# Weight sums moved one block earlier, second-layer weight halves fetched first, token tiles spread: an attention recurrence with two MLPs on one core

## The chip, the cores and the metric

One Trainium2 chip, of which the kernel uses one core. The metric is device microseconds of one execution, as the median of several runs. Lower is better.

## The reference

A linear-attention recurrence feeds a first MLP with a leaky rectifier, and that feeds a second, gated MLP:

```python
for t in range(S):                      # B=4, H=8, S=768, D=48
    cur = einsum('bhd,bhe->bhde', u * k[t], v[t])
    y[t] = einsum('bhd,bhde->bhe', r[t], state + cur)
    state = w * state + einsum('bhd,bhe->bhde', k[t], v[t])
x = y.transpose(0, 2, 1, 3).reshape(3072, 384)
h = x @ w_in                            # 384 -> 2048
x = (maximum(h, 0) + alpha * minimum(h, 0)) @ w_out      # 2048 -> 384
out = ((x @ w1) * (x @ w2)) @ w3 @ w_out2     # 384 -> 1024 -> 1024 -> 384
```

The weights arrive as 64-bit floats. The kernel converts them on the chip into a high and a low 32-bit half, and every product of the MLPs is made of three matmuls (high by high, low by high, high by low), in the helper `mm3` (L123 to L126).

## The kernel before, in words

**Blocks.** The 768 time steps are cut into 6 blocks of 128 steps. With 4 batches that is 512 columns a block, the width of nearly every matmul. A block holds 4 units of attention (a unit is a pair of heads). While the first MLP works on block i, the attention units of block i+1 are woven into its steps.

**The order of the work is written by hand.** A block of the first MLP has 16 steps f, one for each 128 of the 2048 hidden channels. Lists of words say what is issued in a step: `P` is `product1` (9 matmuls into one of two PSUM banks `ph`), `r` is `relus` (two ScalarE passes that free the bank), `s` is `slope` (VectorE), `hl` is `halves` (a ScalarE cast and a GpSimd subtraction, through `split` L120, L121), and `D3` is `down1` of three steps earlier (9 matmuls into `acc`). The list `MIDDLE` (blocks 1 to 4, a period of 4 steps, one attention unit in each period) also holds the words of attention; the list `LAST` (block 5, where no attention is left) is `hl1 P r s D3 xx`. Every engine runs its own instructions in the order in which they were issued, and SP, which issues nearly all DMAs, is one such queue too.

**The word `xx`** runs the function `extra` once in each step of the last block, and all that prepares the second MLP stands in it:

- `mix_load`, `mix`, `mix_store` (L460 to L483): for each of 8 groups of channels two loads of 256 KB, six VectorE operations that make sums and differences of weights, a split into halves by ScalarE and GpSimd, and four stores. The second MLP needs these sums because it forms its products by a scheme that saves matmuls.
- `fetch_o2(k)` (L485 to L494): one of 8 pieces of the second `w_out`, 384 KB each, with both of its halves.
- `fetch_3(j)` (L496 to L503): 1 MB of w3, as tiles `w3h` (of the pool tag "rk", two buffers) and `w3l`; `fold(j)` (24 matmuls of 384 columns into `pf`) multiplies it with all 8 pieces of `w_out`, so that w3 and `w_out` become one matrix; `folded(j)` splits the result `m`. The folds lie in the steps 4 to 11. The two `fetch_3` of the first folds are issued as the block begins, the others two folds ahead.
- `fetch_12(q)` (L451 to L453): weights w of the second MLP, 384 KB, into the buffer of a `w_in` tile that is used up.
- `load_x2`, `x_sum`, `x_cast`, `x_low`, `x_both` (L655 to L716): token tiles of the second MLP (`xr`), their sums (`xsum`, of the tag "rk" as well) and halves (`x`, `xc`), 6 of them ahead of the second MLP's first products.

**The second MLP**, `second`, follows. Its products into the banks `pq` stand in `times` (L753); a copy `t<-pq` (L774) by ScalarE frees the first bank.

**A block's attention** ends with `put_h` and `put_l`, which turn a unit's output y into the halves x, and `put_done`, whose two DMAs `x<-e` (L366) bring them in place. The unit's tiles `rk` and `nat` are loaded by L173 and L174.

The few lines that set the order:

```python
LAST = ("hl1 P r s D3 xx",)
...
words = (MIDDLE, MIDDLE, MIDDLE, MIDDLE, LAST)[i - 1]
for word in words[f % len(words)].split():
```

Of the kernel before, what the change touches and what calls it, by code (L numbers as in the profile page):

```python
# [7 lines left out]
F32 = mybir.dt.float32  # L8
F32R = mybir.dt.float32r
# [8 lines left out]
P = 128  # L18
C = 128
NB = S // C  # L20
NHP = H // 2
N = B * C
DM = H * D
KD = DM // P
F1 = 2048
F2 = 1024
M1 = F1 // P
M2 = F2 // P
# [40 lines left out]
AHEAD2 = ("x11", "x00-x11", "x01+x11", "x00", "x21", "x20")  # L69
# [3 lines left out]
def tile_kernel(ctx: ExitStack, tc: tile.TileContext, a: dict, out: bass.AP):  # L73
    nc = tc.nc
# [4 lines left out]
    gp = ctx.enter_context(tc.tile_pool(name="gp", bufs=GB))  # L79
    ld = ctx.enter_context(tc.tile_pool(name="ld", bufs=2))  # L80
    wk = ctx.enter_context(tc.tile_pool(name="wk", bufs=1))
    st = ctx.enter_context(tc.tile_pool(name="st", bufs=4))
    cv = ctx.enter_context(tc.tile_pool(name="cv", bufs=2))
# [35 lines left out]
    def split(dst_h, dst_l, src, lo=None):  # L119
        nc.scalar.copy(out=dst_h, in_=src)  # L120
        (lo or nc.gpsimd).tensor_tensor(out=dst_l, in0=src, in1=dst_h.bitcast(F32), op=ALU.subtract)  # L121
# [267 lines left out]
    parts = {}  # L389
# [38 lines left out]
    wo2 = {}  # L428
# [22 lines left out]
    def fetch_12(q):  # L451
        w2s[q] = x = wts.tile([P, 2, KD, P], F32R, tag=f"wi{q % M1}", name=f"w12_{q}")
        nc.sync.dma_start(out=x.bitcast(F32).rearrange("p s c m -> p (s c m)"), in_=s12[q % SLOTS])  # L453

    mixes = {}

    def seen(f, j, c0, c1):
        return s12[3 * f + j].rearrange("p (s c m) -> p s c m", s=2, c=KD)[:, :, c0:c1]

    def mix_load(f):  # L460
        mixes[f] = parts = [wk.tile([P, 2, 2, P], F32, tag="rs", name="mix", bufs=2) for j in range(2)]
        for j in range(2):
            nc.sync.dma_start(out=parts[j], in_=seen(f, j, 0, 2))

    def mix(f):
        parts = mixes[f]
        t, o = (wk.tile([P, 4, P], F32, tag=x, name="mix") for x in ("ks", "q1"))
        op = nc.vector.tensor_tensor
        for j in range(2):
            op(out=t[:, 2 * j:2 * j + 2], in0=parts[j][:, 0], in1=parts[j][:, 1], op=ALU.add)  # L470
        w00, w01, w10, w11 = (t[:, m] for m in range(4))
        op(out=o[:, 0], in0=w11, in1=w10, op=ALU.subtract)
        op(out=o[:, 1], in0=o[:, 0], in1=w01, op=ALU.add)
        op(out=o[:, 2], in0=o[:, 1], in1=w00, op=ALU.subtract)
        op(out=o[:, 3], in0=w01, in1=w11, op=ALU.add)
        mixes[f] = h, l = [gp.tile([P, 4, P], F32R, tag="o", name="mix", bufs=3) for _ in range(2)]
        split(h, l, o)

    def mix_store(f):
        for s, x in enumerate(mixes.pop(f)):  # L480
            x = x.bitcast(F32)
            nc.sync.dma_start(out=seen(f, 2, 0, KD)[:, s], in_=x[:, 0:KD])
            nc.sync.dma_start(out=seen(f, 1, 1, 2)[:, s], in_=x[:, KD:])  # L483

    def fetch_o2(k):  # L485
        if k < 7:
            pool, tag, bufs = ((st, "raw", 4), (wk, "am", 2), (wk, "e", 1))[(k >= 4) + (k >= 6)]
            x = pool.tile([P, 2, DM], F32R, tag=tag, name=f"wo2{k}", bufs=bufs)
            nc.sync.dma_start(out=x.bitcast(F32).rearrange("p s m -> p (s m)"), in_=so2[k])
            wo2[k] = x[:, 0], x[:, 1]  # L490
        else:
            wo2[k] = [cv.tile([P, DM], F32R, tag="t", name=f"wo2{k}") for _ in range(2)]
            for m, x in enumerate(wo2[k]):
                nc.sync.dma_start(out=x.bitcast(F32), in_=so2[k, :, m * DM:(m + 1) * DM])  # L494
        ready.add(("o2", k))

    def fetch_3(j):
        w3[j] = (
            ld.tile([P, M2, P], F32R, tag="rk", name="w3h"),
            ld.tile([P, M2, P], F32R, tag="nat", name="w3l"),  # L500
        )
        for m, x in enumerate(w3[j]):
            nc.sync.dma_start(out=x.bitcast(F32).rearrange("p k m -> p (k m)"), in_=s3[j, :, m])  # L503
        ready.add(("w3", j))

    late = [False]
# [138 lines left out]
    def folded(j):  # L645
        m = wts.tile([P, 2, DM], F32R, tag=f"wo{j}", name=f"m{j}")
        split(m[:, 0], m[:, 1], pfs.pop(j), nc.vector)
        ms[j] = m
# [3 lines left out]
    xr = {}  # L652
    xs = {}

    def load_x2(p):  # L655
        for c in range(KD):
            tag, bufs = ("am", 2) if c < 2 else ("e", 1)
            xr[p, c] = raw = wk.tile([P, 2, N], F32, tag=tag, name="xr", bufs=bufs)
            nc.sync.dma_start(out=raw, in_=x2d[2 * p:2 * p + 2, :, c].rearrange("b p n -> p b n"))

    NAMES = ("x11", "x00-x11", "x01+x11", "-x10-x11", "x00+x01", "x00+x10", "x00", "x21", "x20")
# [19 lines left out]
    def x_part(p, x):  # L681
        return xr[p, int(x[1])][:, int(x[2])]

    def x_sum(p, name):
        k = NAMES.index(name)
        if k in (1, 3, 5):
            xt2[p, k] = ld.tile([P, 2, N], F32, tag="rk", name="xsum")
        s = xt2[p, k] if k in (1, 3, 5) else xt2[p, k - 1]
        s = s[:, k in (2, 4)]
        xs[p, name, "sum"] = s  # L690
        if name[0] == "-":
            nc.vector.scalar_tensor_tensor(
                out=s, in0=x_part(p, name[1:4]), scalar=-1.0, in1=x_part(p, name[5:]), op0=ALU.mult, op1=ALU.subtract
            )
        else:
            nc.vector.tensor_tensor(
                out=s, in0=x_part(p, name[:3]), in1=x_part(p, name[4:]), op=ALU.add if name[3] == "+" else ALU.subtract
            )

    def x_cast(p, name):  # L700
        src = x_part(p, name) if len(name) == 3 else xs.pop((p, name, "sum"))
        h, l = xs[p, name] = x_home(p, NAMES.index(name))
        nc.scalar.copy(out=h, in_=src)  # L703
        xs[p, name, "src"] = src

    def x_low(p, name, e=None):
        h, l = xs[p, name]
        (e or nc.gpsimd).tensor_tensor(out=l, in0=xs.pop((p, name, "src")), in1=h.bitcast(F32), op=ALU.subtract)

    def x_both(p, name, e=None):  # L710
        if len(name) > 3:
            x_sum(p, name)
        x_cast(p, name)
        x_low(p, name, e)
# [110 lines left out]
    def second():  # L825
        for k in range(NB // 2 * M2):
# [32 lines left out]
            if f == 3 and p + 1 < NB // 2:  # L859
                load_x2(p + 1)  # L860
# [128 lines left out]
    with tc.manual_schedule():  # L989
# [11 lines left out]
        for x in LOADS.split():  # L1001
            if x[0] == "a" and int(x.rstrip("*")[1:]) in QPE:
                continue
            k = x.rstrip("*")
# [40 lines left out]

        def extra(x):
            f = x % M1
            if f % 2:
                mix(f // 2)
            else:  # L1050
                if f:
                    mix_store(f // 2 - 1)
                mix_load(f // 2)
            if f:
                fetch_12(f - 1)
            if f < 4:
                fetch_o2(2 * f)
                fetch_o2(2 * f + 1)
            j = f - 4
            if 0 <= j < M2:  # L1060
                fold(j)
                folded(j)
                if j + 2 < M2:
                    fetch_3(j + 2)
            if f == 12:
                load_x2(0)
            if f >= 13:
                for x in AHEAD2[2 * f - 26:2 * f - 24]:
                    x_both(0, x, nc.vector if x in ("x00-x11", "x00", "x20") else None)

        table = {k: once(k, unit(fn)) for k, fn in dict(
            q=prep_q, rs=scale_r, ks=scale_k, red=bonus, am=diag, S=scores, fill=fill, Y=out_y, kk=prep_k2,
# [3 lines left out]
            P=product1, r=relus, s=slope, hl=halves, D=down1,  # L1076
# [9 lines left out]
        for word in STARTUP.split():  # L1086
            name = word.rstrip("0123456789")
            table[name](int(word[len(name):] or 0))
        for x in range(M1, STOP or NB * M1):
            i, f = divmod(x, M1)  # L1090
            if (i, f) == (1, 0):
                todo.extend(second_weights())
                issue(1)
                examine()
            if (i, f) == (NB - 1, 0):
                assert not (todo or pend or any(work_in.values())), (len(todo), len(pend), {k: len(v) for k, v in work_in.items()})
                late[0] = True
                fetch_3(0)
                fetch_3(1)
            words = (MIDDLE, MIDDLE, MIDDLE, MIDDLE, LAST)[i - 1]  # L1100
            for word in words[f % len(words)].split():
                name = word.rstrip("0123456789")
                k = int(word[len(name):] or 0)
                if name in per_unit:
                    table[name]((x + AHEAD) // 4 + k)
                elif name in ("P", "r", "s", "hl", "D"):
                    if x - k >= 0:
                        table[name](x - k)
                else:
                    table[name](x)  # L1110
        if STOP:
            return
        table["hl"](NB * M1 - 1)
        mix_store(M2 - 1)
        fetch_12(M1 - 1)
        for f in range(M1 - 3, M1):
            for c in range(KD):
                queue.append(lambda f=f, c=c: down(NB - 1, f, wo[f], M1, x2d, (c,)))
# [89 lines left out]
```

## Time and profile before

| what | us |
|---|---|
| median of 3 runs | 846.4 |
| lowest and highest run | 845.62 and 849.02 |
| the profiled execution, its own time | 851.37 |
| its span in the trace | 849.6 |
| PE (TensorE) busy | 820.8 (97%) |
| VectorE busy | 528.3 (62%) |
| GpSimd busy | 419.0 (49%) |
| ScalarE busy | 357.5 (42%) |

The span runs from the first to the last instruction of the profiled execution; its own time is 1.8 us longer. PE's matmuls are pipelined, so that a busy PE may still be slower than it could be: the granted clock says whether it ran at full speed, and it was 0.983 of that over the span. Times below are microseconds from the start of the span.

### The profile page before, as it was taken

The numbers are of one execution on the slowest core, as the hardware profiler recorded it, in microseconds if no ns is written. First come the engines' busy times: TensorE is split into PE (matmuls) and PEld (weight loads), VectorE is DVE, ScalarE is ACT, GpSimd is POOL, SyncE is SP. The second block draws the span as 40 slices with busy tenths as digits, with TensorE's granted clock in tenths as the row PEclk, the third lists the DMA queues.
The fourth block names the chain that finished last, engine by engine and source line by source line (L and its number), as shares of the span: only waits on it lengthen the run. The fifth ranks groups of instructions, "written<-read, shape, count | busy, mean of one in ns | idle before, by whom it ended". The sixth has DMA issues, their size and how long they took to land. (4 is left out here: it accounts for less than half of the span.)

```text
span 849.6 us, 13555 instructions
## 1 busy us (share of the span) xinstructions
PE 820.8 (97%) x4910; PEld 675.5 (80%) x4910; DVE 528.3 (62%) x883; ACT 357.5 (42%) x703; POOL 419.0 (49%) x339
## 2 busy tenths in 40 slices
PE   8899999999999999999997999979999999999995
PEld 7777788888888888888886899768888888888884
DVE  5889998888787887844324223564467545674442
ACT  4477766555555555543343232431224222332221
POOL 3768876766577667555522122552245322442221
PEclk9999999999999999999999899999999999999998
DMA  8656675766677677732245775734423553242002
GB/s 248 176 183 188 206 216 157 257 208 233 227 214 213 183 225 211 208 130 69 81 143 177 241 243 190 240 100 148 156 93 118 174 186 108 83 168 89 1 0 80
DMA packets 62959, 139.52 MB, mean 164 GB/s; under 512 B 7137, under 2 KB 23522, under 8 KB 62882
## 3 DMA queue, kind: packets, MB, share of 16 engines
q1 hardware_dynamic: 62050, 137.24, 51.2%
q10 hardware_dynamic: 832, 1.31, 0.5%
q8 instruction: 41, 0.67, 0.3%
q14 instruction: 36, 0.29, 0.1%
HBM read 104.15 MB, written 31.46 MB: 160 GB/s over the span
## 5 line engine op out<-in xcount | busy, mean ns | idle before, releaser
L121 POOL TENSOR_TENSOR gl<-g,gh 128x512 fp32r<-128x512 f32 x96 | 129.1, 1345 | 144.1 <-ACT gh L120 143.8
L121 POOL TENSOR_TENSOR gl<-t,gh 128x512 fp32r<-128x512 f32 x48 | 72.2, 1507 | 169.3 <-PE pq L753 144.8
L764 DVE TENSOR_TENSOR t<-pq,t 128x512 f32<-128x512 f32 x96 | 66.1, 688 | 95.5 <-PE pq L753 94.3
L589 DVE SCALAR_TENSOR_TENSOR g<-g,keep,p 128x512 f32<-128x512 f32 x80 | 75.1, 939 | 71.2 <-ACT p L584 70.5
L124 PE MATMUL ph<-x,wi 128*128 128x512 f32 x288 | 116.5, 404 | 1.5 <-DMA x<-e 1.5
L753 PE MATMUL pq<-x,w 128*128 128x512 f32 x408 | 111.3, 390 | 5.9 <-ACT t L774 4.5
L125 PE MATMUL ph<-x,wi 128*128 128x512 f32 x288 | 114.1, 396 | 1.2 <-POOL wi L150 1.2
L124 PE MATMUL acc<-gh,wo 128*128 128x512 f32 x288 | 114.7, 398 | 0.0
L126 PE MATMUL ph<-x,wi 128*128 128x512 f32 x288 | 113.4, 394 | 0.0
L125 PE MATMUL acc<-gh,wo 128*128 128x512 f32 x288 | 112.4, 390 | 0.0
L126 PE MATMUL acc<-gl,wo 128*128 128x512 f32 x288 | 112.4, 390 | 0.0
L753 PE MATMUL pq<-xc,w 128*128 128x512 f32 x384 | 107.9, 393 | 0.0
L753 PEld LDWEIGHTS pq<-x,w 128*128 128x128 f32 x408 | 76.3, 188 | 22.8 <-ACT t L774 4.9
L120 ACT CAST gh<-t 128x512 fp32r<-128x512 f32 x48 | 29.9, 624 | 140.1 <-DVE t L764 140.1
L753 PEld LDWEIGHTS pq<-xc,w 128*128 128x128 f32 x384 | 72.6, 189 | 15.9 <-DVE t L764 0.6
L120 ACT CAST gh<-g 128x512 fp32r<-128x512 f32 x96 | 59.3, 619 | 52.5 <-DVE g L589 51.5
L583 ACT ACTIVATE g<-ph 128x512 f32<-128x512 f32 x96 | 57.1, 595 | 55.3 <-PE ph L126 53.3
L124 PEld LDWEIGHTS ph<-x,wi 128*128 128x128 f32 x288 | 54.8, 190 | 15.0 <-DMA x<-e 1.9
L125 PEld LDWEIGHTS ph<-x,wi 128*128 128x128 f32 x288 | 55.0, 191 | 12.7 <-POOL wi L150 2.2
L124 PEld LDWEIGHTS acc<-gh,wo 128*128 128x128 f32 x288 | 54.4, 189 | 12.7 <-issue 1.0
L126 PEld LDWEIGHTS ph<-x,wi 128*128 128x128 f32 x288 | 54.9, 191 | 11.7
L126 PEld LDWEIGHTS acc<-gl,wo 128*128 128x128 f32 x288 | 54.2, 188 | 11.5
(139 smaller groups left out, 1482.4 us busy)
## 6 DMA issues: line engine op xcount, KB each, us to landing
w<-s SPq DMA_DIRECT2D x72, 384.0 KB, 4.3
raw<-in_wA SPq DMA_DIRECT2D x32, 384.0 KB, 3.8
s<-raw SPq DMA_DIRECT2D x32, 384.0 KB, 3.8
nat<-in_nat SPq DMA_DIRECT2D x20, 576.0 KB, 7.1
rk<-in_rkT SPq DMA_DIRECT2D x20, 448.0 KB, 6.6
raw<-in_wB SPq DMA_DIRECT2D x16, 384.0 KB, 5.3
raw<-in_w3T SPq DMA_DIRECT2D x16, 384.0 KB, 4.0
x2d<-o SPq DMA_DIRECT2D x18, 256.0 KB, 2.1
```

Of the source, the lines that this page charges most:

```text
L120: nc.scalar.copy(out=dst_h, in_=src)
L121: (lo or nc.gpsimd).tensor_tensor(out=dst_l, in0=src, in1=dst_h.bitcast(F32), op=ALU.subtract)
L124: nc.tensor.matmul(out=o, lhsT=wh, rhs=xh, start=first, stop=False)
L125: nc.tensor.matmul(out=o, lhsT=wl, rhs=xh, start=False, stop=False)
L126: nc.tensor.matmul(out=o, lhsT=wh, rhs=xl, start=False, stop=last)
L583: nc.scalar.activation(out=g, in_=ph, func=ACTF.Relu, scale=-1.0)
L589: nc.vector.scalar_tensor_tensor(out=g, in0=g, scalar=alpha[:, f:f + 1], in1=p, op0=ALU.mult, op1=ALU.add)
L753: nc.tensor.matmul(out=o, lhsT=u, rhs=v, start=first and n == 0, stop=last and n == 2, skip_group_check=True)
L764: nc.vector.tensor_tensor(out=o, in0=x, in1=y, op=how)
```

## The change

1. The weight sums leave `extra`. They are issued in block 4 (the fifth block) now, behind the words of each step: the store of the group before and the load in an even step, the arithmetic in an odd one. All their tiles come from the pool of the weights' conversion ("raw", four buffers, idle from the first steps of block 4 on); before, they came from buffers of attention. The store of the last group stands in the first step of block 5.
2. The 8 pieces of `w_out` are all fetched in the first two steps of block 5, pieces 4 to 7 in the first, 0 to 3 in the second. Before, two were fetched in each of the first four steps.
3. `fetch_12` of a step's own weights is issued in that step, not in the next.
4. The token tiles are loaded in the steps 5 and 12 (before: 12), and three of the six are summed, cast and split in the steps 6 to 9, the others in the steps 12, 14 and 15 (before: all six in the steps 13 to 15). GpSimd makes all of their low halves.
5. The block's outputs take their buffers from other tags only from step 2 on (`late`).

```diff
     def mix_load(f):
-        mixes[f] = parts = [wk.tile([P, 2, 2, P], F32, tag="rs", name="mix", bufs=2) for j in range(2)]
+        mixes[f] = parts = [st.tile([P, 2, 2, P], F32, tag="raw", name="mix") for j in range(2)]
...
     def mix(f):
         parts = mixes[f]
-        t, o = (wk.tile([P, 4, P], F32, tag=x, name="mix") for x in ("ks", "q1"))
+        t, o = (st.tile([P, 4, P], F32, tag="raw", name="mix") for _ in range(2))
...
-        mixes[f] = h, l = [gp.tile([P, 4, P], F32R, tag="o", name="mix", bufs=3) for _ in range(2)]
+        mixes[f] = h, l = [st.tile([P, 4, P], F32R, tag="raw", name="mix") for _ in range(2)]
...
     def fetch_o2(k):
-        if k < 7:
-            pool, tag, bufs = ((st, "raw", 4), (wk, "am", 2), (wk, "e", 1))[(k >= 4) + (k >= 6)]
-            x = pool.tile([P, 2, DM], F32R, tag=tag, name=f"wo2{k}", bufs=bufs)
+        if k < 5:
+            x = st.tile([P, 2, DM], F32R, tag="raw", name="wo2") if k < 4 else wk.tile([P, 2, DM], F32R, tag="e", name="wo2")
...
-            wo2[k] = [cv.tile([P, DM], F32R, tag="t", name=f"wo2{k}") for _ in range(2)]
+            pool, tag, bufs = ((cv, "t", 2), (wk, "rs", 2), (wk, None, 1))[k - 5]
+            wo2[k] = [pool.tile([P, DM], F32R, tag=tag or t, name="wo2", bufs=bufs) for t in ("ks", "q1")]
...
-    def load_x2(p):
-        for c in range(KD):
+    def load_x2(p, cs=range(KD)):
+        for c in cs:
...
         def extra(x):
             f = x % M1
-            if f % 2:
-                mix(f // 2)
-            else:
-                if f:
-                    mix_store(f // 2 - 1)
-                mix_load(f // 2)
-            if f:
-                fetch_12(f - 1)
-            if f < 4:
-                fetch_o2(2 * f)
-                fetch_o2(2 * f + 1)
+            if f == 0:
+                mix_store(M2 - 1)
+            fetch_12(f)
+            for k in ((4, 5, 6, 7), (0, 1, 2, 3))[f] if f < 2 else ():
+                fetch_o2(k)
+            if f == 2:
+                late[0] = True
...
+            if f == 5:
+                load_x2(0, (0, 1))
+            if f in (6, 7):
+                x_sum(0, NAMES[f - 5])
+            if f in (7, 8, 9):
+                x_cast(0, NAMES[f - 7])
+                x_low(0, NAMES[f - 7])
             if f == 12:
-                load_x2(0)
-            if f >= 13:
-                for x in AHEAD2[2 * f - 26:2 * f - 24]:
-                    x_both(0, x, nc.vector if x in ("x00-x11", "x00", "x20") else None)
+                load_x2(0, (2,))
+            if f in (12, 14, 15):
+                x_both(0, {12: "x00", 14: "x21", 15: "x20"}[f])
...
             if (i, f) == (NB - 1, 0):
-                late[0] = True
                 fetch_3(0)
                 fetch_3(1)
...
+            if i == NB - 2:
+                if f % 2:
+                    mix(f // 2)
+                else:
+                    if f:
+                        mix_store(f // 2 - 1)
+                    mix_load(f // 2)
...
-        mix_store(M2 - 1)
-        fetch_12(M1 - 1)
```

SP's queue where the last block begins. `wo` are the pieces of `w_out` (a piece in one load of 768 columns, or its halves in two of 384), `w_` the weights of the second MLP, `s_108` their home in memory, `x2d<-o` a block's output. Before:

```order
L489 DMA wo_5066<-so_109 128x768
L489 DMA wo_5068<-so_109 128x768
L626 DMA x2d<-o 128x512 x3
L482 DMA s_108<-mix 128x384
L483 DMA s_108<-mix 128x128
L482 DMA s_108<-mix 128x384
L483 DMA s_108<-mix 128x128
L463 DMA mix<-s_108 128x2x256 x2
L453 DMA w_1_5115<-s_108 128x768
L489 DMA wo_5117<-so_109 128x768
L489 DMA wo_5119<-so_109 128x768
```

And now:

```order
L453 DMA w_0_5176<-s_108 128x768
L488 DMA wo_5178<-so_109 128x768
L494 DMA wo_5180<-so_109 128x384
L494 DMA wo_5181<-so_109 128x384
...
L453 DMA w_1_5220<-s_108 128x768
L488 DMA wo_5222<-so_109 128x768
L488 DMA wo_5224<-so_109 128x768
L488 DMA wo_5226<-so_109 128x768
L488 DMA wo_5228<-so_109 128x768
L626 DMA x2d<-o 128x512 x3
```

The fifth piece of `w_out` (`wo_5117`) stood behind the block's output and a store and load of weight sums; now no such row stands among the pieces.

VectorE in the last block, where `m` is a fold's result, `g` a step of the first MLP and `xsum` a token sum. Now:

```order
L121 TENSOR_TENSOR m_5485<-pf,m_5485 128x384
L696 TENSOR_TENSOR xsum<-xr 128x512
L589 SCALAR_TENSOR_TENSOR g<-g,keep,p 128x512
L121 TENSOR_TENSOR m_5549<-pf,m_5549 128x384
L696 TENSOR_TENSOR xsum<-xr 128x512
L589 SCALAR_TENSOR_TENSOR g<-g,keep,p 128x512
L121 TENSOR_TENSOR m_5615<-pf,m_5615 128x384
```

These sums stood behind all the folds before, and came last with the weight sums in between; `m_5485` is the third fold's result, `m_5549` the fourth's and `m_5615` the fifth's, so that a tile of the tag "rk" is now taken by a sum while folds still need w3 in that tag's two buffers.

ScalarE in block 4, with the numbers of the tiles: `p` is the second of the two passes that free a bank `ph`, `gh` the cast of a step's high half. Before:

```order
L584 ACTIVATE p_4459<-ph_4448 128x512
L120 CAST gh_4477<-g_4458 128x512
L583 ACTIVATE g_4497<-ph_4485 128x512
L584 ACTIVATE p_4498<-ph_4485 128x512
L120 CAST gh_4535<-g_4497 128x512
```

And now:

```order
L584 ACTIVATE p_4483<-ph_4472 128x512
L120 CAST mix_4509<-mix_4502 128x512
L120 CAST gh_4513<-g_4482 128x512
L583 ACTIVATE g_4533<-ph_4521 128x512
L584 ACTIVATE p_4534<-ph_4521 128x512
L120 CAST gh_4579<-g_4533 128x512
```

In every second step of block 4 the cast of a weight sum now stands ahead of the step's own cast and of the next step's two passes that free a bank.

## Rows read from the trace of the kernel before

**Rows 1.** The waits of PE, longest in total first (total, times, longest)

```profile
PE pf L124 <- DMA wo<-so: 6.3, 2, 5.4
PE pq L753 <- ACT t L774: 4.5, 1, 4.5
...
PE pq L753 <- ACT p L584: 1.5, 1, 1.5
```

**Rows 2.** Stretches of 25 us (start:end length, PE, PEld, DVE, ACT, POOL busy, PE's clock, DMA share, GB/s)

```profile
400.00:425.00 25.00, 25.00 (x190) 20.15 (x189) 10.36 (x19) 9.02 (x16) 13.90 (x10) 1.00 0.23 74
...
450.00:475.00 25.00, 18.74 (x72) 15.50 (x71) 7.13 (x11) 6.20 (x13) 6.69 (x6) 0.81 0.73 241
...
525.00:550.00 25.00, 24.03 (x112) 20.27 (x110) 11.89 (x21) 10.96 (x21) 10.92 (x9) 1.00 0.62 203
550.00:575.00 25.00, 20.04 (x80) 16.06 (x81) 16.18 (x24) 8.84 (x16) 12.55 (x9) 0.93 0.36 119
```

**Rows 3.** The timeline of PE at the folds (start, us; in brackets the wait before)

```profile
458.61 0.34 PE L124 MATMUL pf<-wo,w3h 128*128 128x384 f32 x1
...
477.49 0.34 PE L124 MATMUL pf<-wo,w3h 128*128 128x384 f32 x1
...
485.75 0.34 PE L124 MATMUL pf<-wo,w3h 128*128 128x384 f32 x1
```

**Rows 4.** Stretches of 4 us at the first fold, columns as in rows 2

```profile
464.00:468.00 4.00, 1.78 (x6) 1.64 (x6) 1.56 (x1) 1.39 (x3) 2.48 (x2) 0.66 0.99 338
468.00:472.00 4.00, 3.10 (x10) 2.50 (x9) 0.00 (x0) 0.27 (x1) 0.00 (x0) 0.50 0.85 277
```

**Rows 5.** The timeline of PE where the second MLP begins

```profile
548.18 0.84 PE L753 MATMUL pq<-x,w 128*128 128x512 f32 x3
...
556.62 0.96 PE L753 MATMUL pq<-x,w 128*128 128x512 f32 x3 [4.45 <-ACT t L774]
...
563.14 0.84 PE L753 MATMUL pq<-x,w 128*128 128x512 f32 x3
```

**Rows 6.** The timeline of ScalarE there

```profile
553.91 0.62 ACT L120 CAST mix<-mix 128x512 fp32r<-128x512 f32 x1 [3.46 <-DVE mix L475]
```

**Rows 7.** The timeline of VectorE there: a weight sum's first and last operation

```profile
551.95 0.74 DVE L470 TENSOR_TENSOR mix<-mix 128x256 f32<-128x256 f32 x2
...
553.59 0.28 DVE L475 TENSOR_TENSOR mix<-mix 128x128 f32<-128x128 f32 x1
```

**Rows 8.** The timeline of SP's queue in the last block (start, us to issue)

```profile
459.61 0.90 SPq L489 DMA_DIRECT2D wo<-so  x2
...
490.10 0.33 SPq L503 DMA_DIRECT2D w3h<-s  x1
...
499.25 0.38 SPq L482 DMA_DIRECT2D s<-mix  x1
...
501.20 1.51 SPq L463 DMA_DIRECT2D mix<-s  x2
```

**Rows 9.** The tile w3h: its 8 loads

```profile
DMA to landing us min/median/max: 3.5/4.6/5.6
```

**Rows 10.** The tile w3l: its 8 loads

```profile
DMA to landing us min/median/max: 3.0/5.3/7.2
```

**Rows 11.** The line L463 (loads of weight sums), from 531 to 546 us

```profile
DMA to landing us min/median/max: 3.0/3.4/4.3
```

**Rows 12.** The line L463, all of its 16 loads

```profile
DMA to landing us min/median/max: 3.0/4.3/5.9
```

**Rows 13.** The timeline of PE in block 4: a product and the next period's

```profile
388.87 0.39 PE L124 MATMUL ph<-x,wi 128*128 128x512 f32 x1
...
408.38 0.39 PE L124 MATMUL ph<-x,wi 128*128 128x512 f32 x1
```

**Rows 14.** The timeline of SP's queue in block 4

```profile
376.81 1.34 SPq L366 DMA_DIRECT2D x<-e  x2
```

**Rows 15.** The timeline of GpSimd where the second MLP begins: a weight sum's low half

```profile
554.66 1.27 POOL L121 TENSOR_TENSOR mix<-mix 128x512 fp32r<-128x512 f32 x1 [3.18 <-issue]
```

## The prediction

> **What bounds the kernel now.** I first read the waits of PE, then PE's clock by stretches, then the timelines of the two places that stand out. PE is busy 97% of the span, so only what makes PE wait, or run slowly, can change the time. Three waits lie in what the change touches [rows 1]: 6.3 us for pieces of `w_out` in two waits, the longest 5.4, and 4.5 and 1.5 us where the second MLP begins. The stretches show what such waits cost beside themselves: PE's granted clock is 1.00 in block 4 and up to 550, but 0.81 from 450 to 475 and 0.93 from 550 to 575 [rows 2]. Behind the first fold's wait it stood at 0.66 and then at 0.50, which is 1.2 of 2.4 GHz [rows 4]. So each of these two places costs its wait and the slow matmuls behind it, and I price them by start times, not by waits.
>
> *Place A, the first fold.* Two folds are 8.26 us apart where nothing is late (477.49 to 485.75), which is 24 matmuls of the fold and 18 of the first MLP. From the first fold (458.61) to the second (477.49) it is 18.88 us [rows 3]. The loss is 10.6 us. Its cause is in SP's queue: pieces 4 and 5 went out only at 459.61, one us after the fold had begun [rows 8], because the block's output and a store of weight sums, which wait for other engines, stood ahead of them.
>
> *Place B, where the second MLP begins.* From 548.18 to 563.14, 14.96 us, PE did 30 matmuls of 512 columns. A fold period gives the undisturbed pace: in 8.26 us 24 x 384 + 18 x 512 columns pass, 2232 a us, so 30 x 512 take 6.9 us. The loss is 8.1 us. The long wait of 4.45 us [rows 5] is for a copy by ScalarE, which stood behind the cast of the last weight sum, and that cast waited 3.46 us for VectorE [rows 6], whose sum ran from 551.95 to 553.87 [rows 7].
>
> **The change part by part.**
>
> *Pieces of `w_out` in two steps, weight sums out of the way: -10.6.* The cause of place A goes, since no wait on another engine's work is left among the pieces except the release of weight buffers in PE's own pace. What is late next is the transfer itself. In the new order w3 for two folds (4 x 512 KB), the last store of sums (512 KB), two loads of weights and eight pieces (10 x 384 KB) go out one behind the other, 6.6 MB. Block 5 begins four products before the first fold, about 442.3; w3 stands behind the last load of sums, whose arithmetic lies in block 4's last step (from about 437.4, a quarter of 19.5 us before): it starts between 434, if that load is out 3.4 us ahead [rows 11], and 442.3; I take 440, for the ring of sums below runs a little late. The DMA engines moved 338 and 277 GB/s when they were nearly full [rows 4]: the last byte lands between 459.5 and 463.8. The fold begins about 459.3 and needs its last-sent piece 9 matmuls, 1.6 us, later. That is a wait of 0 to 3 us; I take **+1.2**, for the rate between the two rows (about 300) lands it at 462.
>
> *Weight sums and token lows out of the junction: -8.1.* No weight sum is left ahead of the copy on ScalarE, and of the token tiles only two stand in the last two steps, with their low halves on GpSimd. VectorE has only the slopes there. I find nothing late next: the first of them has a whole step, 4.1 us, before PE wants it, and the second is wanted last among the first group's products. The 1.5 us wait goes with it, and the clock's loss too.
>
> *Token sums among the folds: a new wait.* The `xsum` tile takes one of the two buffers of the tag "rk", so from the fifth fold on w3h has one. Before, w3h for fold 4 went out at 490.10 [rows 8], when fold 2 had ended (485.75 and 24 x 384 columns at 2232 a us, 4.1 us, is 489.9) [rows 3], more than a period early. Now the loads for folds 5 and 6 wait for the end of folds 4 and 5, and only the 18 matmuls of the first MLP, 4.1 us, cover them. A load of w3h lands in 3.5 to 5.6 us [rows 9]; w3l goes out about 0.4 us behind it and lands in 3.0 to 7.2, 5.3 at the median [rows 10], and the fold wants it at its second matmul. So each of the two folds starts 0.4 + 5.3 - 4.1 - 0.2 = 1.4 to 1.5 us late at the median; the bounds are 0 (3.5 is under 4.1) and 3.3 (7.2). I take **+3.0** for both, bounds 0 and 6.6. The wait of 1.5 us before the second MLP left the clock at 1.00 (525 to 550) [rows 1, 2], so I add nothing for it. The Trainium skill prices one transfer otherwise: "DMA: Bandwidth & Descriptors", section "Anatomy of one DMA", fits for the path that GpSimd issues 2.0 us plus the bytes at 436 GB/s. By that the pair of 1 MB would take an estimated 4.4 us, the two waits would be under 0.2 us each, and the sum 2.7 us lower. The trace does not agree: w3l alone, half as large, took 5.3 at the median [rows 10].
> VectorE's first token sum must wait for the end of fold 3 too, and a slope and fold 3's result stand behind it. Three operations of at most 512 columns, at 0.74 us for 512 [rows 7], and a cast of 0.6 [rows 6] are about 2.8 of the 4.1 us to the next fold, so I cost this at nothing. If they need more, fold 4 starts late by the difference.
>
> *Weight sums in block 4: another new wait.* PE waited for nothing there, its clock was 1.00 and the DMA engines moved 74 GB/s [rows 2], so there is room, but the sums now run in a ring. From the end of ScalarE's cast, GpSimd's low half takes 1.3 us [rows 15], the second pair of stores behind it 0.95 of SP and the two loads 1.5, the second of them out halfway (all from 499.25 to 502.71) [rows 8]; it lands 3.4 us later [rows 11], VectorE needs 1.9 [rows 7] and the next cast 0.6 [rows 6]. A round is 1.4 + 0.95 + 0.75 + 3.4 + 1.9 + 0.6 = 9.0 us. Two rounds must fit in a unit's period of 19.5 us (388.87 to 408.38) [rows 13], with the two `x<-e` of 1.3 us on the same queue [rows 14]: 19.3 of 19.5. It just fits, with waits in the in-order queues of VectorE (the fill of a unit) and ScalarE on top. Where the ring is late, the cast of a sum holds back the two passes behind it on ScalarE, these free a bank, and PE waits with its next product but one. Nothing in the trace shows this ring, so I bound it: 0 if the slack holds; at the 4.3 us median of all such loads [rows 12] each round is 0.9 longer, 8 rounds lose 7. I take **+2**, nearer to the low end, because the 3.4 is from a stretch at about 203 GB/s [rows 2], which is what 74 and the sums' own 8 MB in 78 us (105) come near to.
>
> *At nothing:* the weights' loads one step earlier (each still follows the product that frees its buffer), the token loads at step 5 (their data were written blocks earlier), the other buffers for outputs. They are hidden by PE's own 8.3 us steps; if a load were late there, a fold or a product would wait for SP, as above.
>
> The sum: -10.6 - 8.1 + 1.2 + 3.0 + 2 = -12.5. The profiled execution took 851.4, 5 us over the median of 846.4; against it the forecast is 838.9, and for the median **833.9**.
>
> **The rivals.**
>
> *No new wait decides.* The loads land early enough and the ring holds: 846.4 - 18.7 = 827.7. For it speaks the shortest landing of w3h, 3.5; against it the median of w3l. Chance 0.17.
>
> *The `w_out` pieces stay late.* If the queue of 6.6 MB is slower than 277 GB/s, or starts later than 440, the first fold waits 5 us again, 4 more than forecast, and the clock falls behind it, which cost 10.6 - 6.3 = 4.3 before; half of that, since the wait is split, makes 6 more: 840. For it speaks that the DMA engines' share was 0.99 [rows 4]; against it that the fold wants eight pieces spread over 4 us. Chance 0.12.
>
> *The junction keeps a wait.* The last two tiles, both behind slopes' lows on GpSimd, come late by half of what the old chain took, about 4 us: 838. Chance 0.08.
>
> *The ring becomes the bound* (this one ends slower). Place: block 4, the loads of sums, which now run beside the units' own loads. At the longest landing seen, 5.9 us [rows 12], each round is 2.5 us longer than with 3.4, and 8 rounds cost 20 more than I forecast: 833.9 + 20 = 854. It decides over all gains once a round takes 8 x (r - 9.7) = 18.7 - 4.2, that is from about 11.5 us on. For it: the ring has no slack by my count. Against it: the load is light there. Chance 0.05.
>
> **How the numbers follow.** The forecast's own case has 0.58 and lies between 829 and 839. The range goes from 827 (no new wait) to 842: the forecast with the ring at its upper bound (+5) and both w3 waits at theirs (+3.6) would be 842.5; it takes in the late pieces at 840 and leaves out the ring as the bound. A measurement of this kernel can tell about 0.5%, 4.2 us, from no change: faster ends at 842.2, slower begins at 850.6. Faster: all but the ring and the ends of the middle cases, 0.87; within: 0.09; slower: 0.04.
>
> **What would show it.** In the changed profile: the waits of PE for `wo` under 3 us in all; the clock from 450 to 475 at 0.95 or more; the wait for the copy `t` gone, the clock where the second MLP begins at 1.00; two waits of PE for w3h or w3l of 1 to 2 us each at the sixth and seventh folds; in block 4 a few waits of PE for ScalarE's `p` of under 1 us, on a ring of about 9.7 us from store to store. I am wrong if PE's waits in block 4 add up to over 7 us, if the first fold still waits over 4, or if the second MLP begins with a wait of over 2 us.

## The result and the profile after

The changed kernel takes 838.7 us (median of 4 runs, 837.71 to 839.84), against 846.1 before: a ratio of 0.9906, with a 95% interval of 0.9879 to 0.9933, so 7.4 us faster. The forecast was 833.9, 12.5 us below the 846.4 known then. Measured again with the experiments below it took 841.1 (12 runs, 835.92 to 847.81), a ratio of 0.9943 (0.9917 to 0.9969), so that the gain is 5.8 to 7.4 us. Its profiled execution took 838.0, with a span of 836.2.

The waits of PE in the changed kernel, longest in total first (total, times, longest; those of the kernel's start are left out):

```profile
PE ph L124 <- ACT p L584: 3.1, 2, 1.7
...
PE py L351 <- DVE am L308: 1.3, 2, 0.6
...
PE pf L125 <- DMA w3l<-s: 1.1, 2, 0.8
```

All three waits of [rows 1] are gone from the top: none for `wo`, none for the copy `t`. What came in their place are two waits for `p`, two for `am` (the fill of an attention unit) and two for w3l. The stretches tell where:

```profile
400.00:425.00 25.00, 22.69 (x177) 17.89 (x176) 14.81 (x27) 7.94 (x15) 15.77 (x11) 1.00 0.52 156
425.00:450.00 25.00, 22.90 (x123) 18.49 (x123) 15.60 (x32) 11.35 (x22) 10.43 (x8) 1.00 0.56 181
450.00:475.00 25.00, 24.88 (x120) 21.52 (x120) 5.27 (x8) 9.68 (x20) 6.44 (x5) 1.00 0.85 306
...
525.00:550.00 25.00, 25.00 (x113) 20.87 (x112) 7.87 (x11) 11.83 (x22) 12.35 (x10) 1.00 0.27 85
550.00:575.00 25.00, 25.00 (x112) 20.69 (x112) 12.48 (x19) 6.06 (x11) 8.07 (x6) 1.00 0.39 127
```

Against [rows 2] the clock is at 1.00 throughout, and the stretch of the first fold has 24.9 us of work instead of 18.7. Block 4 (400 to 450), which had been full, lacks 4.4 us. The starts of the folds on PE's timeline (the first, second, third, sixth, seventh and eighth, with the two waits):

```profile
461.15 0.34 PE L124 MATMUL pf<-wo,w3h 128*128 128x384 f32 x1
...
470.01 0.34 PE L124 MATMUL pf<-wo,w3h 128*128 128x384 f32 x1
...
478.32 0.34 PE L124 MATMUL pf<-wo,w3h 128*128 128x384 f32 x1
...
503.24 0.34 PE L124 MATMUL pf<-wo,w3h 128*128 128x384 f32 x1
503.93 0.44 PE L125 MATMUL pf<-wo,w3l 128*128 128x384 f32 x1 [0.35 <-DMA w3l<-s]
...
512.37 0.41 PE L124 MATMUL pf<-wo,w3h 128*128 128x384 f32 x1
513.55 0.45 PE L125 MATMUL pf<-wo,w3l 128*128 128x384 f32 x1 [0.77 <-DMA w3l<-s]
...
521.80 0.34 PE L124 MATMUL pf<-wo,w3h 128*128 128x384 f32 x1
```

From the first to the second fold it is 8.86 us, against 18.88 in [rows 3]; an undisturbed period is 8.31 here. From the sixth to the seventh it is 9.13, and to the eighth 9.43. Block 4's first new waits on PE's timeline, and the second wait for `p`, one unit later:

```profile
407.66 0.50 PE L124 MATMUL ph<-x,wi 128*128 128x512 f32 x1 [1.67 <-ACT p L584]
...
410.63 1.08 PE L351 MATMUL py<-rs,state 112*64 112x128 f32 x16 [0.63 <-DVE am L308]
...
429.64 0.50 PE L124 MATMUL ph<-x,wi 128*128 128x512 f32 x1 [1.47 <-ACT p L584]
```

The `py` of one unit and the next lay 19.51 us apart before (391.00 to 410.51) and lie 22.35 apart here (388.28 to 410.63), then 21.98 (to 432.61): 2.8 and 2.5 us lost, 5.3 in all.

### The profile page after: what moved, and what is told of

The parts are those of the page before. It is cut to its first block, busy times and chain, and to the rows that moved or that the text cites. A ratio compares the mean times of both kernels' runs of the same rounds, so it can differ in the third digit from the quotient of the medians.

```text
span 836.2 us, 13560 instructions
## 1 busy us (share of the span) xinstructions
PE 814.5 (97%) x4910; PEld 669.9 (80%) x4910; DVE 529.6 (63%) x880; ACT 355.7 (43%) x703; POOL 422.6 (51%) x342
## 4 chain that ended last, share of the span: by engine, by line
PE 77%; DMA 7%; DVE 5%; issue 3%; POOL 3%; ACT 2%; SPq 2%; DVEq 0%; POOLq 0%; ACTq 0%
PE pq L753 21%; PE acc L124 8%; PE acc L125 7%; PE acc L126 7%; PE ph L124 6%; PE ph L125 6%; PE ph L126 6%; PE py L357 2%; PE py L351 2%; PE acb L126 2%; PE acb L124 2%; PE acb L125 2%; DMA mix<-s 2%; DMA wo<-so 1%; PE pf L125 1%
## 5 line engine op out<-in xcount | busy, mean ns | idle before, releaser
L121 POOL TENSOR_TENSOR gl<-g,gh 128x512 fp32r<-128x512 f32 x96 | 126.5, 1318 | 118.2 <-ACT gh L120 115.2
L589 DVE SCALAR_TENSOR_TENSOR g<-g,keep,p 128x512 f32<-128x512 f32 x80 | 78.6, 983 | 61.5 <-ACT p L584 58.1
L124 PEld LDWEIGHTS ph<-x,wi 128*128 128x128 f32 x288 | 54.1, 188 | 18.7 <-ACT p L584 4.3
L124 PEld LDWEIGHTS acc<-gh,wo 128*128 128x128 f32 x288 | 54.1, 188 | 12.5 <-issue 1.1
L125 PEld LDWEIGHTS ph<-x,wi 128*128 128x128 f32 x288 | 54.1, 188 | 12.4 <-POOL wi L150 2.2
L126 PEld LDWEIGHTS ph<-x,wi 128*128 128x128 f32 x288 | 54.1, 188 | 11.5
```

The costliest lines, as they stand in the source:

```text
L124: nc.tensor.matmul(out=o, lhsT=wh, rhs=xh, start=first, stop=False)
L125: nc.tensor.matmul(out=o, lhsT=wl, rhs=xh, start=False, stop=False)
L126: nc.tensor.matmul(out=o, lhsT=wh, rhs=xl, start=False, stop=last)
L589: nc.vector.scalar_tensor_tensor(out=g, in0=g, scalar=alpha[:, f:f + 1], in1=p, op0=ALU.mult, op1=ALU.add)
```

## The experiments

**e1, the kernel before once more, without an edit.** The forecast had been built on one profile, of an execution 5 us over its median.

> The kernel before, unchanged, for a second profile of it. The first profiled execution took 851.4 us, 5 more than the median of the runs. Theory: the places that the change removes cost the same in each execution (10.6 us at the first fold, 8.1 where the second MLP begins), and what varies is the start, where the granted clock was 0.86 and 0.93 in the first two stretches of 25 us: then this profile shows the same two losses within 0.5 us and, if it takes about 846, a faster start. Rival: the losses themselves vary, since a wait of 5 us may or may not pull the clock down behind it: then one of the two is smaller by 2 to 4 us here, and the gain of the change is smaller than the first profile says.

It took 845.25 us. Its start is faster: the granted clock reads 1.00 in the first two stretches of 25 us (0.86 and 0.93 before), and the fifth group `py` stands at 51.61 instead of 54.13, from where on the two run alike up to the folds. The first fold's waits on PE's timeline (the first, the two waits and the second fold):

```profile
456.06 0.34 PE L124 MATMUL pf<-wo,w3h 128*128 128x384 f32 x1
...
461.55 0.61 PE L124 MATMUL pf<-wo,w3h 128*128 128x384 f32 x1 [3.24 <-DMA wo<-so]
...
465.25 0.69 PE L124 MATMUL pf<-wo,w3h 128*128 128x384 f32 x1 [1.44 <-DMA wo<-so]
...
472.00 0.34 PE L124 MATMUL pf<-wo,w3h 128*128 128x384 f32 x1
```

15.94 us instead of 18.88: the loss is 7.7 here, not 10.6. From the last fold to the last matmul it is 312.5 us against 313.1 in the first profile and 305.2 in the changed kernel, so that the second MLP's beginning lost 7.9 and 7.3. Both theories held in part: of the 6.1 us between the two profiled executions the start accounts for 2.5 and the first fold for 2.9. The loss at the first fold is not the same in each execution; which of the two values is nearer to that of a median run, two profiles do not show.

**e2, the token sums in another buffer.**

```diff
-        if k in (1, 3, 5):
-            xt2[p, k] = ld.tile([P, 2, N], F32, tag="rk", name="xsum")
+        if p == 0 and k < 3:
+            s = gp.tile([P, N], F32, tag="o", name="xsum", bufs=3)
```

> The changed kernel, with the first two token sums in buffers of the tag "o" (free then), so that w3h keeps both buffers of "rk". Theory (the buffer makes folds 5 and 6 wait): the periods from fold 5 to 6 and from 6 to 7, 9.13 and 9.43 us in the changed kernel, go to 8.3 as the others, no wait for w3l is left, and the time falls by 2.0, to about 836.7. Rival (the w3 loads are late because the token loads run beside them): the two waits stay, within 0.3 us, and the time stays at 838.7.

836.3 us (6 runs, 835.11 to 838.73), a ratio of 0.9879 (0.9856 to 0.9902), whose interval overlaps that of the changed kernel's first measurement (0.9879 to 0.9933); the periods decide, not the time. No wait for w3l is left, and the last three folds stand at:

```profile
502.53 0.34 PE L124 MATMUL pf<-wo,w3h 128*128 128x384 f32 x1
...
510.84 0.34 PE L124 MATMUL pf<-wo,w3h 128*128 128x384 f32 x1
...
519.14 0.34 PE L124 MATMUL pf<-wo,w3h 128*128 128x384 f32 x1
```

Periods of 8.31 and 8.30. The cause is seen in SP's queue as well: in the changed kernel the load for the sixth fold went out at 499.31, the very end of the fifth, and here at 490.29, a period earlier. First the changed kernel, then this run:

```profile
499.31 0.32 SPq L503 DMA_DIRECT2D w3h<-s  x1
```

```profile
490.29 0.32 SPq L503 DMA_DIRECT2D w3h<-s  x1
```

The token loads still run, so the rival falls. Block 4, which this edit leaves alone, keeps its long unit periods (21.89 and 21.85).

**e3, one store and load of weight sums moved ahead of x<-e.**

```diff
+            if i == NB - 2 and f % 4 == 2:
+                mix_store(f // 2 - 1)
+                mix_load(f // 2)
             words = (MIDDLE, MIDDLE, MIDDLE, MIDDLE, LAST)[i - 1]
...
-                else:
+                elif f % 4 == 0:
```

> The changed kernel, with the store of an even group of weight sums and the load of the next odd one issued ahead of the step's words instead of behind them, in the steps that hold x<-e; nothing else moves. Theory (SP's order: the stores are ready at about 371, but stand behind x<-e, which goes out at 374, and the load of the odd group lands too late for its sum): the two waits of 1.7 and 1.5 us for the pass p and the two of 0.6 for the fill go, the two unit periods of 22.4 and 22.0 us fall to 19.5 to 20, and the time falls by 4 to 5.3, to about 834. Rival (the sums cost what they take of VectorE, ScalarE, GpSimd and the DMA engines, wherever they stand): the periods stay at 22 and the time at 838.7.

832.5 us (5 runs, 830.52 to 835.06), a ratio of 0.9829 (0.9803 to 0.9855). The unit periods are 19.51 and 19.51, as before the change, and no wait for `p` is left. The first fold loses nothing either: its period is 8.31. Stretches of 20 us, of the changed kernel and then of this one:

```profile
390.00:410.00 20.00, 18.32 (x110) 13.96 (x104) 12.09 (x20) 6.79 (x13) 11.76 (x9) 1.00 0.46 139
410.00:430.00 20.00, 17.90 (x129) 14.45 (x130) 12.20 (x24) 7.48 (x15) 13.51 (x10) 1.00 0.33 99
```

```profile
390.00:410.00 20.00, 20.00 (x150) 16.32 (x148) 14.80 (x26) 7.94 (x15) 14.32 (x11) 1.00 0.52 166
410.00:430.00 20.00, 20.00 (x150) 16.31 (x147) 14.62 (x29) 8.03 (x16) 11.74 (x9) 1.00 0.35 112
```

The same work on VectorE, ScalarE, GpSimd and the DMA engines fits without a wait, so it was not too much work, but its order on one queue. The chain in the changed kernel, row by row: ScalarE's cast of the even group's sum stands at 393.81, so its first store could go out at about 394.5; but on SP it stood behind `x<-e`, which waits for the unit's own result. VectorE finishes that at about 396.16, and SP goes on behind it:

```profile
395.47 0.69 DVE L398 TENSOR_TENSOR x<-py,x 112x512 fp32r<-112x512 f32 x1 [1.69 <-ACT x L394]
```

```profile
396.19 1.33 SPq L366 DMA_DIRECT2D x<-e  x2
397.57 0.58 SPq L482 DMA_DIRECT2D s<-mix  x1
...
399.66 1.23 SPq L463 DMA_DIRECT2D mix<-s  x2
```

In this run the same three are in the other order, and the load goes out 4.6 us earlier: 2.9 by the order, and 1.7 because the cast stands earlier too (392.06), since the load before it had also gone out earlier (384.6 instead of 386.2):

```profile
392.70 0.33 SPq L482 DMA_DIRECT2D s<-mix  x1
...
395.02 1.18 SPq L463 DMA_DIRECT2D mix<-s  x2
396.29 1.32 SPq L366 DMA_DIRECT2D x<-e  x2
```

What the late load held up in the changed kernel, on VectorE and on ScalarE:

```profile
402.75 0.43 DVE L470 TENSOR_TENSOR mix<-mix 128x256 f32<-128x256 f32 x1 [2.11 <-DMA mix<-s]
403.85 0.43 DVE L470 TENSOR_TENSOR mix<-mix 128x256 f32<-128x256 f32 x1 [0.67 <-DMA mix<-s]
```

```profile
405.49 0.62 ACT L120 CAST mix<-mix 128x512 fp32r<-128x512 f32 x1 [6.19 <-DVE mix L475]
406.02 0.61 ACT L120 CAST gh<-g 128x512 fp32r<-128x512 f32 x1
406.54 0.59 ACT L583 ACTIVATE g<-ph 128x512 f32<-128x512 f32 x1
407.02 0.59 ACT L584 ACTIVATE p<-ph 128x512 f32<-128x512 f32 x1
```

ScalarE idled 6.19 us with the step's two passes ready behind that cast; the second of them ends at 407.6, and PE starts at 407.66.

**e4, the token tiles as before the change.**

```diff
-            if f == 5:
-                load_x2(0, (0, 1))
...
             if f == 12:
-                load_x2(0, (2,))
+                load_x2(0)
+            if f >= 13:
+                for x in AHEAD2[2 * f - 26:2 * f - 24]:
+                    x_both(0, x, nc.vector if x in ("x00-x11", "x00", "x20") else None)
```

> The changed kernel, with the token tiles loaded, summed and split as before: all in the steps 12 to 15, three of their low halves on VectorE. Theory: the waits of folds 5 and 6 for w3 go (-2.0), and where the second MLP begins a part of the old loss of 8.1 comes back, since the sums of the weights, which held ScalarE's copy up longest, are no longer there but the token chain is: 2 to 4 us; the time is 839 to 841. Rival a (the token chain alone made the old loss): 8 come back, 845. Rival b (the weight sums alone made it): nothing comes back, 836.7, and spreading the token tiles brought nothing.

838.4 us (5 runs, 836.71 to 839.40). The waits for w3 are gone. From the last fold to the last matmul it is 305.6 us, 0.4 more than in the changed kernel, with one wait of 0.5 us for the copy `t`: at this place rival b is right and the theory's 2 to 4 us did not come back. The weight sums alone had made the old loss, and spreading the token tiles is worth 0.4 us. The time did not fall by the 2 us of the folds. In the profile, the slowest of the five runs, block 4, which this edit leaves alone, lost more: unit periods of 24.69 and 21.15. Whether it did in the other runs is not shown. One load of sums landed late:

```profile
405.98 0.42 DVE L470 TENSOR_TENSOR mix<-mix 128x256 f32<-128x256 f32 x1 [2.33 <-DMA mix<-s]
```

```profile
409.79 0.50 PE L124 MATMUL ph<-x,wi 128*128 128x512 f32 x1 [3.28 <-ACT p L584]
```

**e5, the order of the fetches alone, on the kernel before.**

```diff
-            if f < 4:
-                fetch_o2(2 * f)
-                fetch_o2(2 * f + 1)
+            for k in ((0, 1, 2, 3), (4, 5, 6, 7))[f] if f < 2 else ():
+                fetch_o2(k)
```

> The kernel before, with one part of the change: the 8 pieces of w_out are fetched in the first two steps of the last block (0 to 3, then 4 to 7), in the buffers of before; the weight sums and token tiles stay where they were. Theory (the pieces were late only because SP held them behind the block's output and a store of sums): the first fold's loss, 10.6 and 7.7 us in two profiles, falls under 2, the loss of 7 to 8 where the second MLP begins stays, and the time is 838 to 840. Rival (the sums' own traffic and waits make the pieces late wherever they stand): over 4 us of the loss stay, and the time is 842 to 845.

839.7 us (6 runs, 838.84 to 841.33), 0.9925 (0.9905 to 0.9945). The first two folds:

```profile
457.43 0.34 PE L124 MATMUL pf<-wo,w3h 128*128 128x384 f32 x1
...
465.68 0.34 PE L124 MATMUL pf<-wo,w3h 128*128 128x384 f32 x1
```

8.25 us: this one edit recovers the whole loss of place A, and the 4.5 us wait for `t` stays. With 7.1 us it gains as much as the whole change (5.8 measured beside it, 7.4 before).

**e6, the weight sums alone, on the kernel before.** The edits are those of the diff to `mix_load`, `mix`, the branch in block 4 and the last store; `fetch_o2`, `fetch_12` and the token tiles are those of before.

> The kernel before, with one part of the change: the weight sums are made in block 4 in the conversions' buffers, as in the changed kernel; w_out is fetched two pieces a step, and the token tiles are made in the last steps, as before. Theory: block 4 loses 5 us, the first fold loses 1 to 3 (pieces 4 to 7 still go out behind the block's output), no fold waits for w3, and where the second MLP begins 0.5 is left; the time is 836 to 840, about that of the changed kernel, with which it shares all but the two smaller parts. Rival (the order of the fetches was what the first fold needed): its loss stays at 7 or more and the time is 843 or more.

835.1 us (6 runs, 834.73 to 838.98), 0.9879 (0.9855 to 0.9902). The first fold loses 1.9 us, with one wait for a piece of `w_out` of 1.2; no fold waits for w3; block 4's periods are 21.75 and 22.19, 4.9 us lost; from the last fold to the end it is 305.0 us, so that nothing of place B is left. The moved sums alone gain 11.8 us, more than the whole change (5.8 measured beside it), and their intervals do not overlap. What the rest of the change took back is shown only in part: the folds' 2.0 us, against 1.0 to 1.3 given at the first fold. In the profiles the last matmul ends at 826.2 here, at 827.4 in the changed kernel and at 829.1 in e7; the other 2.0 and 2.8 us between the spans lie behind it (6.9 us here, 8.8 and 9.7 there), where the last outputs are stored and no edit reaches.

**e7, the changed kernel once more.**

> The changed kernel, unchanged, for a second profile and for its time beside these. Theory (block 4's loss is a ring whose loads are waited for, so it moves with when a load of sums lands): the two long unit periods differ from 22.4 and 22.0 by up to 2 us, the two waits for w3l stay at 0.3 to 1, and the time is 837 to 841. Rival (a fixed cost): the periods repeat within 0.2.

841.1 us (12 runs, 835.92 to 847.81). Unit periods of 24.37 and 20.97, against 22.35 and 21.98: the cost of block 4 is not a fixed one. The second sum's second operand was late again:

```profile
405.32 0.43 DVE L470 TENSOR_TENSOR mix<-mix 128x256 f32<-128x256 f32 x1 [1.97 <-DMA mix<-s]
```

```profile
409.13 0.78 PE L124 MATMUL ph<-x,wi 128*128 128x512 f32 x1 [2.94 <-ACT p L584]
```

Three executions give the price of a late load here. The second load of that group landed in 3.5, 4.8 and 5.2 us (the longest of the two in the changed kernel, in e7 and in e4), and PE waited 1.67, 2.94 and 3.28 for `p`: 1.3 later costs 1.27, 1.7 later 1.61. That is one for one, as on a chain with no slack. The profiles of e6 and e2 lie on the same line: 3.1 and 3.2 us to landing, and waits of 1.21 and 1.27. The periods lost 2.8, 4.9 and 5.2, more than the wait, since the fill waits as well, or the clock falls (last section).

**e8, the edits of e2 and e3 together.**

> The changed kernel with the edits of the runs e2 and e3 together: token sums in buffers of the tag "o", and the store and load of weight sums ahead of the words in the steps that hold x<-e. Theory (two separate waits): the gains add, 2.0 below the 832.5 of the load ahead, about 830.5; no wait of PE over 0.6 us is left between 370 and 560, and fold periods are 8.3. Rival (what is saved at one place is lost at the next): 832 or more.

830.25 us (5 runs, 828.44 to 831.44), 0.9804 (0.9782 to 0.9827): 16.6 us under the kernel before on the same chip (846.85), and the best of all. Between 370 and 560 us PE waits for nothing; the stretches from 400 on:

```profile
400.00:425.00 25.00, 25.00 (x189) 20.15 (x189) 18.64 (x31) 10.49 (x20) 17.07 (x12) 1.00 0.40 132
425.00:450.00 25.00, 25.00 (x135) 20.57 (x134) 12.64 (x26) 13.11 (x25) 10.95 (x9) 1.00 0.75 252
450.00:475.00 25.00, 25.00 (x126) 22.44 (x125) 4.12 (x6) 6.97 (x13) 4.44 (x4) 1.00 0.77 278
```

The two gains add: 832.5 to 830.25, 2.3 where 2.0 was expected, though the two series of runs overlap (830.52 to 835.06, 828.44 to 831.44).

## Why the prediction was right in sign and short in size

The direction and its causes held, and 838.7 lies within the range, but the size did not: 12.5 us were forecast and 7.4 came. By the steps:

| step | forecast | measured, from starts on PE's timeline |
|---|---|---|
| first fold, gain | -10.6 | -10.6 and -7.7 in two profiles of before |
| first fold, transfer late | +1.2 | +0.6; 0.9 in e7 |
| where the second MLP begins | -8.1 | -7.9 and -7.3 |
| folds 5 and 6 (counted from 0) | +3.0 | +2.0 (0.83 and 1.13); 2.0 in e7 |
| block 4 | +2 | +5.3; 6.3 in e7 |

With the second profile of before the measured terms give -7.7 + 0.6 - 7.3 + 2.0 + 5.3 = -7.1, beside the medians' -7.4. So two steps failed.

**The term of block 4** was mis-sized: +2, where 5.3 to 6.3 was measured. The step that failed is the one by which two rounds "must fit in a unit's period of 19.5 us", with the two `x<-e` of 1.3 us on the same queue. It counted `x<-e` by the time that SP needs to issue it. What counts is how long it holds the queue: it waits for the unit's result, and the stores behind it, ready at about 394.5, went out at 397.57, 3.1 us late. e3 shows that this was all: with the same work in another order the loss is zero. The landing that I took, 3.4 us, was right in the middle (3.2 at the median), and for the load that goes out at about 400 each us above it came through one for one. The bound had let that happen in all 8 rounds; here one load carried it, while the last load of e4, which landed in 5.8 us, was followed by a wait of 0.4.

**The gain at the first fold** was taken from one execution that lay 5 us above its median; the text said so and set the sum against that execution, but then carried the difference over to the median unchanged. Part of those 5 us was the loss itself (e1). With the second profile's loss the forecast would have been 2.9 us smaller.

The other steps held. Place A was SP's order (e5 alone removes it), place B was the weight sums ahead of ScalarE's copy (e6; the token tiles matter for 0.4 us, e4). The folds waited for the end of the fold before, through the buffer (e2). They lost 2.0 instead of 3.0: w3l landed in 4.2 and 4.9 us, where the median of 5.3 had been taken, and w3h in 3.2 and 4.0, under the 4.1 that cover it. Two signs were missed: the waits for w3l were 0.35 and 0.77 us and not 1 to 2, and those for `p` 1.67 and 1.47 and not under 1. Of the rivals the one that ends slower was the right mechanism at a quarter of its size: the ring did become a bound, but it cost 5 to 6 us in place of 22. The slow end of e7, 847.8, is over the forecast's range; only profiled executions have a trace, so that what that run lost is not shown.

## What to carry to other kernels

An instruction that waits in an in-order DMA queue costs ready work behind it that time (3.1 us here), so count what it waits for and not what it takes to issue; put work that is ready early ahead of it. When a part of the work is moved into idle engines, draw the ring that its buffers and queues make (store, load, sum, cast, store) and find where another chain holds it. And price a loss from at least two profiles of the same kernel (here 10.6 and 7.7 us), above all where a long wait also lowers the clock.

## What was not expected of the hardware

Of PE's waits, those of 1.67 and 1.47 us left the granted clock at 1.00, but behind 2.94 and 3.28 us it fell. The stretches of 4 us around the ends of these two waits, of e7 and of e4:

```profile
408.00:412.00 4.00, 2.87 (x7) 2.31 (x8) 2.85 (x6) 2.08 (x5) 2.72 (x3) 0.65 0.51 169
```

```profile
409.00:413.00 4.00, 3.21 (x9) 2.42 (x9) 3.12 (x6) 2.08 (x5) 2.72 (x3) 0.68 0.55 177
```

In e7 the unit with the wait of 2.94 lost 2.0 us more than that with 1.67, though PE waited only 1.3 more. Half of it came back: the next unit waited 0.45 for `p` instead of 1.47, and block 4 as a whole lost 1.0 more (6.3 against 5.3). The prediction had seen the clock fall only behind 4.5 and 5.4 us.

VectorE's sums of weights took longer beside GpSimd. In the changed kernel two operations of the line L470 took 2.79 us at 389.82 where 0.74 is usual [rows 7], while GpSimd ran two operations on attention's tiles:

```profile
389.82 2.79 DVE L470 TENSOR_TENSOR mix<-mix 128x256 f32<-128x256 f32 x2
```

```profile
389.10 1.79 POOL L193 TENSOR_TENSOR rs<-rk,pw 112x512 f32<-112x512 f32 x1
390.85 1.46 POOL L199 TENSOR_TENSOR ks<-rk,pw 112x512 f32<-112x512 f32 x1
```

The Trainium skill, "SBUF — State Buffer", section "Who interferes with whom", says that a VectorE instruction with two inputs in SBUF contends with a GpSimd instruction that reads SBUF, since its second input comes through a read port that the two share. The rows agree with it, VectorE's pair of operations lasting 2.05 us longer. In e8 such an operation still takes up to 1.49 us in place of 0.42, and PE waits nowhere there. In the changed kernel the slow pair stands in the chain of the late load: the cast of its sum follows at 393.81, the unit's own cast behind that, and `x<-e` at 396.19. What the 2.05 us cost there, no run separates.
